# Routed attention with a SoLU layer on one core: six exponentials in w_in's place and the first part of the queues rewritten

## The chip, the cores and the metric

One core of a Trainium2 chip runs one launch. The metric is the device time in microseconds, as the median of several executions. The kernel before takes 224.04 us (three runs, 223.92 to 224.38).

## What is computed

The reference has two stages. First, attention with a mask by clusters, for 4 batches, 8 heads, 768 tokens and 64 columns per head:

```
q_assign = argmax(q_n @ c_n.T); k_assign = argmax(k_n @ c_n.T)     # 16 centroids a head
scores   = where(q_assign == k_assign, q @ k.T / 8, -1e9)
attn     = softmax(scores); x = attn @ v                            # 4 x 8 heads of 768 x 64
```

Then a feed-forward layer on x, taken as 3072 tokens of 512 columns:

```
h    = x @ w_in                                                     # 512 x 1024
solu = h * softmax(h)
out  = ((solu - mean) / sqrt(var + 1e-6) * g_ln) @ w_out            # 1024 x 512
```

## The kernel before

**How the work is tiled.** Heads are taken in 16 pairs (batch b, pair p). A pair's q and k are cast to bf16 and stored transposed, with 16 or 32 more rows under them that hold the one-hot cluster marks of each token. The product of the two then carries the score and a large constant (BIAS_C) where the clusters agree, so that one exponential gives the masked weights without a search for the maximum. Scores are made bank by bank in PSUM, 128 keys by up to 512 queries, with three banks in turn. ScalarE writes each bank's exponential as a tile e (nine buffers in turn, `ring_e` in line 1016). TensorE then multiplies e with v, which has a column of ones for the denominator, and VectorE divides. Token blocks of 128 rows, 24 in all, go through the feed-forward layer as soon as all their heads are done.

**How the order is set.** Nothing is scheduled by a program at run time. The class Weave (line 23) holds one written-out queue for each engine, `ORDER`, as a list of kinds with counts; `AWAY` names the operations that run on another engine than their usual one. Each `add` (line 98) registers an operation with its name, its engine, a cost in us, and the operations it needs. `run` (line 125) only decides in which sequence the five queues are emitted; on the chip each engine works its own queue strictly in order and waits on semaphores. So an operation that waits holds up everything behind it on its engine.

**The names**, as the steps below use them:

- `tp` (L387) TensorE transposes half of a pair's raw q (i = 0) or k (i = 1); `xa` (L394) keeps the result in SBUF (xt); `xt` (L408) is VectorE's own transpose, for batches 1 to 3.
- `ca` (L432, L434, L436) casts xt to bf16 (qk). For the first pair a cast is half a head, 64x384; for all others it is 64x768.
- `cl` (L446, L451) TensorE computes the cluster scores; `tb` (L460), `mx` (L473), `oh` (L479, L485) and `ot` (L492, L495) on VectorE make the transposed one-hot marks of them; `pl` (L507, L515) copies these marks under q and k; `bl` (L524) blanks rows.
- `S` (L602) scores, `E` (L608) exponentials, `V` (L625) the product with v, `N` (L637, L650) the division, `cv` (L533) the cast of v, `lv` (L528) its load, `ld` the loads of q and k.
- `wm` and `fl` (L820) are TensorE products of zeros that are used for nothing; `cp`, `cq` (L865) transpose the centroids.
- `li`, `wi` (L550, L553) load and cast w_in; `lo` (L566) loads w_out; `su`, `sk`, `me`, `ce` (L575, L582, L585, L588) centre w_out with g.
- for block f: `tx` (L680) transposes x, `h` (L711), `hm` (L717, row maximum), `ex` (L723), `u` (L730), `tu` (L735), `bn`, `ag` (L741, L745), `at`, `al` (L751 to L760), `y` (L775), `sc` (L790, L792), `ou` (L802).

S and E carry unit and bank: pair (0,0) is units 0 to 3, with six banks of 384 columns each (24 banks); units 4 to 21 are the other pairs of batch 0, with three banks of 512; batch 1 begins with unit 22. h3.1.0 is block 3, second half of the columns, first part. It writes over a bank that u2 reads, so it needs u2.

**The first part of the queues**, with the kinds spelled out:

```
PE   wm tp0.0.0.0 tp0.0.1.0 cp tp0.0.0.1 cl0.0.0 tp0.0.1.1 fl x5 cl0.0.1 fl x4 S0.0 S0.1 S0.2 tp0.1.0.0
     tp0.1.0.1 S1.0 S1.1 tp0.1.1.0 S1.2 cq S0.3 tp0.1.1.1 S0.4 S0.5 tp0.2.0.0 tp0.2.0.1 S1.3 S1.4
     V0.0 V0.1 V0.2 S1.5 cl0.1 S2.0 ...
ACT  wa xa0.0.0.0 xa0.0.1.0 ca0.0.0.0.0 ca0.0.0.1.1 xa0.0.1.1 ca0.0.1.0.1 ca0.0.1.1.0
     E0.0-0.2 E1.0-1.2 E0.3-0.5 E1.3-1.5 xa0.2.1.0 xa0.2.1.1 E2.0-2.5 xa0.3.0.0 E3.0 ...
DVE  cn cb xa0.0.0.1 ca0.0.1.0.0 tb0.0.0 mx0.0.0 oh0.0.0 ot0.0.0 pl0.0.0.1.1 pl0.0.0.0.0 tb0.0.1 mx oh ot
     xa0.1.0.0 xa0.1.0.1 xa0.1.1.0 bl0.0.1 cf cv0.0.0 xa0.1.1.1 zo xa0.2.0.0 xa0.2.0.1 tb0.1 ca0.1.1.0
     mx0.1 oh0.1 gk N0 ot0.1 tb0.2 ...
POOL po z1 ca0.0.0.0.1 ca0.0.0.1.0 pl0.0.0.1.0 pl0.0.0.0.1 cv0.0.1 z2 bl0.0.0 ...
SP   ld0.0 x4 lv0.0 si ld0.1.0 ld0.1.1 ld0.2.0 ld0.2.1 lv0.1 lg ld0.3.0 ld0.3.1 ld1.0 x2 lv0.2 lv0.3 ...
```

The tile w_in_sb (line 536) is filled by `wi` only after 38 us. Before that its first columns, 0 to 255 of rows 0 and 1, hold the index pattern for the identity matrix and the normed centroids (lines 812 and 841).

Of the kernel before, what the change touches and what calls it, by code (L numbers as in the profile page):

```python
# [11 lines left out]
BF16 = mybir.dt.bfloat16  # L12
# [10 lines left out]
class Weave:  # L23
# [18 lines left out]
    """
    ORDER["PE"] = """
        wm tp2 cp tp cl tp fl5 cl fl4 S3 tp2 S2 tp S cq S tp S2 tp2 S2 V3 S cl S tp2 V3 S gt S tp S
        tp S2 cl S2 V2 S V S2 tp S2 tp S2 V2 S V S2 cl S2 V2 S V2 S3 V S2 V2 S2 V S cl S3 su S2 V3 S
        V S3 V3 S2 V S su S2 V S V3 S3 me S3 V4 S3 cl S3 V4 S2 h S h S2 h S h S2 V3 S2 V h S h V S V
        S h S V S V S h S2 V3 S2 V h S2 h V2 S y3 S2 h3 S3 y V3 h V S2 V2 S cl S3 h2 S2 V3 S y2 S V
        h2 S V y2 S h S V h S2 h S y3 S2 y V3 h S3 cl V2 S V S y S2 y2 S3 V3 S y S2 V3 S2 cl S V S2
        V2 S h S2 V2 S V S h S2 V2 cl V2 S3 y2 S V S2 V y S2 y V2 S3 h2 S V h S h S2 V h S V S V y2
        S h V y2 S2 V S h3 S cl V S2 V2 S h V cl S3 h2 V y V S3 y2 V S h V3 S y S h S2 h2 S3 V2 y h  # L50
        S V S2 y V3 y S3 h3 y S3 V3 S h S V S V cl S V S h S cl V2 S3 y V2 S y S2 y V2 S3 h y V S3 V
        h V2 S3 cl S2 V2 S y3 S2 y S V3 S V S y S2 V S V3 S2 y2 S3 y V2 S2 h V2 S3 h3 S V S2 V y S V
        h2 V2 S y S2 y V y S h2 S3 cl h V S2 V3 S h V2 S3 h2 S y S2 V h S2 V y2 V4 S3 y h S2 h V h V
        S V S y2 S3 V3 h2 S2 h2 S2 y2 S V S h2 S V3 S2 h S h S2 V S y V2 S V y2 S2 h2 S2 h2 V2 S2 V2
        y S2 h V2 h V S2 h S V h S3 V2 h y S V y3 V h3 S2 y3 S2 y h2 V2 h y h y3 h V h V y4 h ptx h
        y4 h2 y3 h2 y ptu2 y6 ptu y ptu y5
    """
    ORDER["DVE"] = """
        cn cb xa ca tb mx oh ot pl2 tb mx oh ot xa3 bl cf cv xa zo xa2 tb ca mx oh gk N ot tb pl mx
        xa2 oh xa cv N ot tb pl N xt mx xt N oh ot tb pl2 ca N pl xt mx N sk oh N ot xt ce3 N tb ce5  # L60
        N hm mx N u oh ot bn N bn ag hm xt2 u N bn2 hm ag sc xt u N bn tb hm mx bn oh ag u xt bn ot
        xt N cv hm bn ag sc xt tb mx N u xt oh ot sc N bn2 xt ag xt tb N hm mx tb N oh ot u xt mx N
        bn oh bn xt hm ot ag N cv u bn2 xt hm tb mx u N tb oh mx hm ot bn2 oh ag u N sc ag hm bn ot
        u bn N xt2 ag xt2 hm tb N bl mx tb bn2 oh u N xt ag xt sc hm ot tb mx oh N bn sc N u bn N ag
        xt ot bn ca N mx sc oh hm u bn ag N xt hm bn2 bl tb u ot ag N hm mx bn2 u bn N oh ot hm bl2
        u ag N cv hm sc bn u N hm ag bn N bn u bn2 hm ag2 N bn u bn2 N ag hm bn u N ag hm bn2 u bn2
        hm sc u N ag2 bn tx hm bn sc u bn ag hm bn tu ag u2 bn2 ag sc
    """
    ORDER["ACT"] = """
        wa xa2 ca2 xa ca2 E12 xa2 E6 xa E58 ex E12 ex E8 ex E8 ex E3 sc E5 ca E2 ex E25 ex E9 sc E6  # L70
        ex E5 sc E2 ex E9 ex E8 ex E9 sc E6 ex E18 ex E21 ex E5 sc E3 ex E9 ex E7 sc E2 ex E7 ex E8
        ex E7 ex E6 sc E ex E2 sc E3 ex E2 sc ex sc ex sc ex tu sc tu2 sc2 oz
# [97 lines left out]
def kernel(  # L170
# [328 lines left out]
    def place(b, p, hf, i, part, e):  # L499
# [6 lines left out]
        if apart(b, p):  # L506
            ins = VEC[e].tensor_copy(  # L507
                side(b, p, i, part, slice(0, S))[D:D + NC_].bitcast(F32)
                .rearrange("p (t u n) -> p u t n", t=n_t // 2, u=2),
                asg[b, p, hf, "oht"][r.start:r.start + NC_].bitcast(F32)  # L510
                .rearrange("p (u t n) -> p u t n", t=n_t // 2, u=2))
        elif e == "SP":
            ins = nc.sync.dma_start(out=dst, in_=src.unsqueeze(1).to_broadcast([NB, 2, n]))
        else:
            ins = VEC[e].tensor_copy(dst.bitcast(F32), src.bitcast(F32).unsqueeze(1)  # L515
                                     .to_broadcast([NB, 2, n // 2]))
# [76 lines left out]
    es, sps_, opss, xs = {}, {}, {}, {}  # L593

# [10 lines left out]
    def expo(n, k):  # L605
        w = wide(n, k)
        es[n, k] = ep.tile([P, 512], BF16, name="e")
# [203 lines left out]
    load_v(0, 0)  # L811
# [47 lines left out]
    for j in range(sum(int(x or 1) for x in re.findall(r"\bfl(\d*)", wv.ORDER.get("PE", "")))):  # L859
# [41 lines left out]
    for idx, (b, p) in enumerate(pairs):  # L901
# [18 lines left out]
        for i in range(2):  # L920
# [340 lines left out]
```

## Time and profile before

| what | value |
|---|---|
| median of three runs | 224.04 us |
| the execution that was profiled | 223.91 us |
| its span, from first to last instruction | 221.9 us |
| granted TensorE clock | 1.00 |
| TensorE matmul busy | 213.1 us (96%) |
| VectorE busy | 197.2 us (89%) |
| ScalarE busy | 191.7 us (86%) |
| GpSimd busy | 127.1 us (57%) |

Busy shares are averages over stages with different limits. A busy TensorE is not a TensorE at its peak, since the ends of its pipelined matmuls are modelled. A row of the timeline reads: start, length, engine, line, operation, what is written and read, how many instructions were merged, and in brackets how long the engine sat idle before and what it waited for.

### The profile page before, as it was taken

The page shows a single profiled execution, that of the slowest core. Times are in us where ns is not written, and L with a number is a line of the kernel's source. Part 1 is how long each engine was busy: PE and PEld are TensorE (multiplying, and loading weights), DVE is VectorE, ACT ScalarE, POOL GpSimd, SP SyncE. Part 2 cuts the span into 40 slices and gives each one's busy share as a digit, 9 for nine tenths or more (in the row PEclk, how much of TensorE's full clock was granted, in tenths as well). Part 3 has the DMA queues.
Part 4 walks back from the last instruction along what each step waited for, and adds up shares of the span by engine and source line. Part 5 has one row for each costly group of instructions (what it writes and reads, how often), then busy time and mean ns, then how long its engine had stood idle before and what let it go on. Part 6 is the DMA issues. An engine that isn't in the chain of part 4 may idle for free.

```text
span 221.9 us, 6576 instructions
## 1 busy us (share of the span) xinstructions
PE 213.1 (96%) x2388; PEld 146.3 (66%) x2420; DVE 197.2 (89%) x359; ACT 191.7 (86%) x372; POOL 127.1 (57%) x247
## 2 busy tenths in 40 slices
PE   7899999999999999999999999999999999999994
PEld 2575656677667678776577666777677777755452
DVE  3899898899999999999998999887999889888982
ACT  3689999999899999998889899999899998983363
POOL 3499842954794999547668534953895403022331
PEclk9999999999999999999999999999999999999999
DMA  6997999999897989899999898499930524396723
GB/s 150 337 324 157 244 226 296 277 237 161 141 214 134 218 140 168 193 193 173 187 240 150 153 184 207 90 171 240 227 74 11 97 57 135 85 136 166 177 80 142
DMA packets 125679, 38.80 MB, mean 175 GB/s; under 512 B 115016, under 2 KB 121168, under 8 KB 125648
## 3 DMA queue, kind: packets, MB, share of 16 engines
q1 hardware_dynamic: 123904, 37.87, 80.4%
q10 hardware_dynamic: 1744, 0.52, 1.0%
q8 instruction: 19, 0.31, 0.6%
q14 instruction: 12, 0.10, 0.1%
HBM read 23.11 MB, written 6.29 MB: 132 GB/s over the span
## 4 chain that ended last, share of the span: by engine, by line
PE 83%; ACT 6%; issue 3%; DVE 2%; DMA 2%; POOL 1%; SPq 1%; ACTq 0%; DVEq 0%; POOLq 0%
PE sps L602 27%; PE hreg L711 17%; PE yps L775 17%; PE ops L625 13%; ACT e L608 5%; PE csc L451 4%; DMA raw<-in_q_dram 2%; PE hreg L387 1%; PE hreg L575 1%; PE hreg L775 1%; PE csc L446 1%; DVE u L730 1%; SPq L370 0%; PE utp L699 0%; ACT xt L394 0%
## 5 line engine op out<-in xcount | busy, mean ns | idle before, releaser
L608 ACT ACTIVATE e<-sps 128x512 bf16<-128x512 f32 (+1 forms) x294 | 150.7, 601 | 11.6 <-PE sps L602 9.6
L602 PE MATMUL sps<-qk 80*128 80x256 bf16 (+5 forms) x636 | 94.2, 264 | 2.0 <-POOL qk L515 0.7
L602 PEld LDWEIGHTS <-qk 80*128 80x128 bf16 (+1 forms) x636 | 60.3, 121 | 28.3 <-issue 9.2
L625 PEld LDWEIGHTS <-e 128*128 128x128 bf16 x1152 | 49.2, 97 | 12.3 <-issue 1.9
L625 PE MATMUL ops<-v,e 128*128 128x65 bf16 x1152 | 53.5, 193 | 0.1
L711 PE MATMUL hreg<-w_in_sb,xT 128*128 128x512 bf16 x173 | 49.1, 379 | 1.1
L775 PE MATMUL yps<-w_out_c,uT 128*128 128x512 bf16 x171 | 46.6, 379 | 0.6
L730 DVE TENSOR_TENSOR u<-e_sb,hreg 128x1024 bf16<-128x1024 bf16 (+1 forms) x25 | 29.1, 1168 | 4.8 <-ACT e_sb L723 4.5
L515 POOL COPY qk<-oht 32x384 f32<-32x384 f32 (+1 forms) x50 | 24.4, 488 | 15.6 <-DVE oht L495 13.4
L741 DVE BATCH_NORM_STATS2 bs<-u 128x6 f32<-128x512 bf16 x48 | 31.5, 677 | 0.1
L717 DVE TENSOR_REDUCE nmax<-hreg 128x1 f32<-128x1024 f32 x24 | 29.0, 1208 | 2.5 <-PE hreg L711 2.2
L723 ACT ACTIVATE e_sb<-hreg,nmax 128x1024 bf16<-128x1024 f32 x24 | 26.9, 1123 | 4.5 <-DVE nmax L717 4.4
L434 POOL CAST qk<-xt 64x768 bf16<-64x768 f32 (+1 forms) x31 | 25.9, 837 | 4.8 <-DVE xt L394 3.3
L775 PEld LDWEIGHTS <-uT 128*128 128x128 bf16 x200 | 18.2, 97 | 11.7 <-issue 0.3
L757 POOL TENSOR_SCALAR esq<-es,mv 128x1 f32<-128x1 f32 x24 | 8.5, 355 | 28.9 <-DVE mv L745 20.7
L436 POOL TENSOR_SCALAR qk<-xt 64x768 bf16<-64x768 f32 (+1 forms) x28 | 22.8, 815 | 1.7
L711 PEld LDWEIGHTS <-xT 128*128 128x128 bf16 x192 | 16.7, 97 | 9.5 <-DVE u L730 0.6
L408 DVE STREAM_TRANSPOSE xt<-raw 128x768 f32<-128x768 f32 x24 | 22.7, 953 | 0.2 <-DMA w_g<-in_moe_w_out_dram 0.2
L751 POOL TENSOR_SCALAR es<-esum 128x1 f32<-128x1 f32 x24 | 5.3, 222 | 27.5 <-ACT e_sb L723 27.0
L650 DVE TENSOR_TENSOR x<-ops,den 128x256 bf16<-128x256 f32 (+1 forms) x39 | 19.0, 486 | 1.3
L760 POOL TENSOR_TENSOR alpha<-esq,halves 128x1 f32<-128x1 f32 x24 | 13.5, 561 | 2.0
L533 POOL CAST v<-vf 128x384 bf16<-128x384 f32 x27 | 13.5, 516 | 0.9 <-DMA vf<-in_v_dram 0.2
(80 smaller groups left out, 165.6 us busy)
## 6 DMA issues: line engine op xcount, KB each, us to landing
vf<-in_v_dram SPq DMA_DIRECT2D x16, 384.0 KB, 4.7
out_dram<-y SPq DMA_DIRECT2D x23, 256.0 KB, 2.6
raw<-in_q_dram SPq DMA_DIRECT2D x50, 96.0 KB, 3.3
raw<-in_k_dram SPq DMA_DIRECT2D x50, 96.0 KB, 2.9
w_g<-in_moe_w_out_dram SPq DMA_DIRECT2D x4, 512.0 KB, 4.6
w_st<-in_moe_w_in_dram SPq DMA_DIRECT2D x4, 512.0 KB, 5.9
raw<-in_q_dram SPq DMA_DIRECT2D x3, 384.0 KB, 6.2
raw<-in_k_dram SPq DMA_DIRECT2D x3, 384.0 KB, 6.7
```

The lines of the kernel that those rows point to most:

```text
L434: VEC[e].tensor_copy(dst, src)
L436: VEC[e].tensor_scalar(dst, src, scalar1=inv_C, scalar2=1.0, op0=Alu.mult, op1=Alu.mult)
L515: ins = VEC[e].tensor_copy(dst.bitcast(F32), src.bitcast(F32).unsqueeze(1) .to_broadcast([NB, 2, n // 2]))
L602: nc.tensor.matmul(sps_[n, k][:, c0:c0 + w], side(b, h // 2, 1, h % 2, keys)[r], side(b, h // 2, 0, h % 2, slice(s0 * P, s0 * P + w))[r])
L608: nc.scalar.activation(es[n, k][:, :w], sps_[n, k][:, :w], Act.Exp, scale=exp_scale, bias=-exp_scale)
L625: nc.tensor.matmul(opss[g][:, s, :VW], es[n, k][:, c0:c0 + P], v1[slot(b, h // 2)][:, h % 2, kt, :VW], start=(kt == 0), stop=(kt == n_t - 1))
L711: uses(nc.tensor.matmul(hreg[:, at(f, f2)[1], :], xTs[f][:, dc, :], w_in_sb[:, dc, f2 * FF2:(f2 + 1) * FF2], start=(dc == 0), stop=(dc == ...
L717: uses(nc.vector.tensor_reduce(ff[f, "nmax"][:], pair_of(f), axis=AXY, op=Alu.max, negate=True), *both(f))
L723: uses(nc.scalar.activation(ff[f, "e"][:], pair_of(f), Act.Exp, bias=ff[f, "nmax"][:], accum_out=ff[f, "esum"][:]), *both(f))
L730: uses(nc.vector.tensor_tensor(ff[f, "u"][:, at_], ff[f, "e"][:, at_], pair_of(f)[:, at_], op=Alu.mult), *banks)
L741: nc.vector.bn_stats(ff[f, "bs"][:, f2, :], ff[f, "u"][:, f2, :])
L775: ins = nc.tensor.matmul(dst, ff[f, "uT"][:, at(f, f2)[0] * (n_fc // 2) + c, :], w_out_c[:, fc, cols], start=(fc == chunks[0]), stop=(fc = ...
```

## The change

The tiles, the shapes and the arithmetic of all operations stay as they are. Five things change.

1. **Six exponentials outside the ring.** The first six E (E0.0 to E0.2, E1.0 to E1.2) are written into free columns 256 to 1023 of rows 0 to 2 of w_in_sb. The nine buffers serve the seventh and later ones, so the sixteenth E is the first that needs an earlier V; before it was the tenth. Each `wi` now also needs `cp`, `cq` and the V of units 0 and 1.
2. **First casts and marks shared out anew.** `place` can run on ScalarE. Before the first score, ScalarE now does two of the first four marks and two casts, in place of four casts; GpSimd does the other two marks, and VectorE none. Later in the head VectorE is given casts that GpSimd did.
3. **Narrower needs.** S of the first pair with keys kt = 0 needs only the first key mark of its half, with kt = 2 only the second. S0.0 is registered after all `fl`, `gs` after all `fl`.
4. **v later or sooner on SP.** lv0.0 leaves the code ahead of the queues and comes after four ld; the others follow one at a time between ld.
5. **New order up to about 60 us** in each queue; behind it the lists are the same word for word (from S26.2 on TensorE, E26.2 on ScalarE, N11 on VectorE, at2 on GpSimd, ld2.0.0.1 on SP).

The new first part of the queues:

```
PE   fl wm fl tp0.0.0.0 fl cp tp0.0.1.0 fl x4 cl0.0.0 tp0.0.0.1 fl tp0.0.1.1 fl cl0.0.1 tp0.1.0.0 S0.0 S0.1 S0.2
     cq tp0.1.0.1 S1.0 tp0.1.1.0 S1.1 tp0.1.1.1 S1.2 S0.3 tp0.2.0.0 S0.4 tp0.2.0.1 S0.5 S1.3 tp0.2.1.0 S1.4
     cl0.1 S1.5 S2.0 V0.0 S2.1 tp0.2.1.1 S2.2 V0.1 S2.3 V0.2 S2.4 V1.0 S2.5 gt V1.1 V1.2 cl0.2 S3.0 ...
ACT  wa xa0.0.1.0 ca0.0.0.0.0 ca0.0.1.0.0 xa0.0.0.1 xa0.0.1.1 pl0.0.0.1.0 pl0.0.0.0.1
     E0.0-0.2 E1.0-1.2 E0.3-0.5 E1.3 ca0.0.0.0.1 E1.4 E1.5 E2.0-2.2 xa0.2.1.0 xa0.2.1.1 E2.3-2.5 E3.0-3.5
     E4.0-4.2 xa0.3.1.1 E5.0 ... E26.1 ca1.1.0.0 E26.2
DVE  cn xa0.0.0.0 cb ca0.0.0.1.0 tb0.0.0 mx oh ot0.0.0 ca0.0.1.0.1 tb0.0.1 mx xa0.1.0.0 oh ot xa0.1.0.1
     xa0.1.1.0 xa0.1.1.1 pl0.0.1.0.1 cf xa0.2.0.0 xa0.2.0.1 tb0.1 mx0.1 ca0.1.1.0 oh0.1 gk ca0.1.1.1 N0 ot0.1
     tb0.2 pl0.1.0.0 xa0.3.0.0 xa0.3.0.1 mx0.2 oh0.2 xa0.3.1.0 N1 ot0.2 tb0.3 cv0.1.1 ca0.2.1.0 N2 ...
POOL sg z1 zo po ca0.0.1.1.0 ca0.0.0.1.1 pl0.0.0.0.0 pl0.0.0.1.1 bl0.0.0 ca0.0.1.1.1 pl0.0.1.1.0 ...
SP   ld0.0 x4 si ld0.1.0 ld0.1.1 ld0.2.0 ld0.2.1 lv0.0 ld0.3.0 ld0.3.1 lg lv0.1 ld1.0 lv0.2 ld1.0 x2 lv0.3 ...
     ... li3 tx0 tx2 ld1.2 x2 lv1.0 ld1.2 x3 lv1.1 ...
```

Between ot0.1 and u2 the VectorE queue swaps one xa for another, gains cv0.1.1, ca0.2.1.0, cv0.3.0, ca1.0.0.0, cv0.3.1, ca1.0.1.0, ca1.0.1.1 and ca1.1.0.1, and loses cv0.2.0, pl0.2.1.1, pl0.3.0.0 and pl0.3.0.1.

The diff, with the queues and lists cut to a few lines:

```diff
     ORDER["ACT"] = """
-        wa xa2 ca2 xa ca2 E12 xa2 E6 xa E58 ex E12 ex E8 ex E8 ex E3 sc E5 ca E2 ex E25 ex E9 sc E6
...
+        wa xa ca2 xa2 pl2 E10 ca E5 xa2 E12 xa E49 ex E10 ex E6 ca E4 ex E8 ex E3 sc E5 ca
...
+        elif e == "ACT":
+            ins = nc.scalar.copy(dst, src.unsqueeze(1).to_broadcast([NB, 2, n]))
...
+    n_lent = 6
+    assert all(wide(*nk) <= HALF for nk in BANKS[:n_lent])
...
-        es[n, k] = ep.tile([P, 512], BF16, name="e")
+        i = BANKS.index((n, k))
+        es[n, k] = (w_in_sb[:, i // 2, 2 * P + i % 2 * HALF:2 * P + (i % 2 + 1) * HALF]
+                    if i < n_lent else ep.tile([P, 512], BF16, name="e"))
...
-    load_v(0, 0)
...
-            add(f"lv{t}", "SP", 0.0, -1990, lambda e: None, [], last_ld[-1:], move=1.3)
+            add(f"lv{t}", "SP", 0.5, first - 34, lambda e: load_v(0, 0), [], ["si"], move=1.3)
...
-            hots = [(i, part) for i in (1, 0) for part in range(2)]
+            hots = ([(1, 0), (0, 0), (0, 1), (1, 1)] if half and not hf else
+                    [(i, part) for i in (1, 0) for part in range(2)])
...
-                   for part in ((hh,) if apart(b, p) else range(2))}
+                   for part in ((hh,) if apart(b, p) else range(2))
+                   if not (halves_of(b, p) and x and kt % 3 == 2 * (1 - part))}
...
-            (lambda e, n=n, k=k: scores(n, k)), nd, ["S{}.{}".format(*BANKS[i - 1])] if i else [])
+            (lambda e, n=n, k=k: scores(n, k)), nd,
+            ["S{}.{}".format(*BANKS[i - 1])] if i else [f"fl{j}" for j in range(n_idle)])
...
-        if i >= ring_e:
+        if i >= ring_e + n_lent:
...
-        add(f"wi{dc}", "POOL", 1.04, 28 + dc, (lambda e, dc=dc: cast_w_in(dc, e)), [f"li{dc}"],
+        add(f"wi{dc}", "POOL", 1.04, 28 + dc, (lambda e, dc=dc: cast_w_in(dc, e)),
+            [f"li{dc}", "cp", "cq"] + [f"V{n}.{j}" for n in GROUPS[0] for j in range(3)],
             also={"DVE": 0.62})
```

More of the change, by code (lines that the diff above doesn't have):

```diff
@@ L52 @@
[L52 to L56, printed above, removed]
+        fl wm fl tp fl cp tp fl4 cl tp fl tp fl cl tp S3 cq tp S tp S tp S2 tp S tp S2 tp S
```

131 lines of the change are left out of this document (73 added, 58 removed).

## The prediction

> **What bounds the kernel now.** I read the shares of the page first, then the chain that ended last, then busy time by stretches that I cut where the limits change.
>
> ```profile
> PE 213.1 (96%) x2388; PEld 146.3 (66%) x2420; DVE 197.2 (89%) x359; ACT 191.7 (86%) x372; POOL 127.1 (57%) x247
> ...
> PE 83%; ACT 6%; issue 3%; DVE 2%; DMA 2%; POOL 1%; SPq 1%; ACTq 0%; DVEq 0%; POOLq 0%
> ```
>
> ```profile
> 0.00:9.68 9.68, 7.39 (x44) 3.59 (x45) 5.11 (x21) 4.79 (x9) 3.60 (x17) 1.00 0.83 224
> ...
> 18.30:26.50 8.20, 7.89 (x110) 5.21 (x109) 7.38 (x16) 7.92 (x19) 7.25 (x13) 1.00 0.82 190
> 26.50:44.00 17.50, 16.96 (x221) 10.42 (x220) 15.84 (x32) 16.62 (x33) 10.40 (x15) 1.00 1.03 258
> 44.00:65.20 21.20, 20.60 (x254) 15.29 (x256) 20.38 (x34) 20.22 (x41) 13.93 (x25) 1.00 1.01 190
> 65.20:120.00 54.80, 54.26 (x606) 38.60 (x615) 52.49 (x90) 51.02 (x99) 38.93 (x70) 1.00 0.99 182
> 18.30:65.20 46.90, 45.45 (x580) 30.92 (x583) 43.59 (x80) 44.75 (x91) 31.58 (x52) 1.00 0.98 215
> ```
>
> The columns are the stretch, its length, then busy PE, PEld, DVE, ACT and POOL. Up to 9.68 us nobody is full: it is one dependent chain from the load of q and k to the first score. From there ScalarE paces (7.92 of 8.20, then 16.62 of 17.50). From 44 us on PE, DVE and ACT are all full: DVE idles 0.82 us of 21.20, PE 0.60. So a lead won in the head reaches the end only if both PE and DVE carry it through 44 to 65 us, where the queues become the old ones. Behind that PE has no idle time to give back and its order is unchanged, so the lead that it has at 65 us is the gain.
>
> **Part 1, the first score (lead 0.05 to 0.3 us, taken 0.2).**
>
> ```profile
> 6.26 0.53 PE L451 MATMUL csc<-xt,c_bd 128*32 128x192 f32 x8
> ...
> 6.37 0.56 DVE L394 COPY xt<-hreg 128x384 f32<-128x384 f32 x1 [0.37 <-PE hreg L387]
> ...
> 6.84 0.34 DVE L436 TENSOR_SCALAR qk<-xt 64x384 bf16<-64x384 f32 x1
> ...
> 7.11 0.37 DVE L460 STREAM_TRANSPOSE cst<-csc 128x192 f32<-128x192 f32 x1
> ...
> 7.88 1.06 ACT L432 ACTIVATE qk<-xt 64x384 bf16<-64x384 f32 x2
> ...
> 8.77 0.58 DVE L515 COPY qk<-oht 32x192 f32<-32x192 f32 x2
> 8.88 0.75 POOL L515 COPY qk<-oht 32x192 f32<-32x192 f32 x2 [0.77 <-DVE oht L495]
> ...
> 9.68 0.65 PE L602 MATMUL sps<-qk 80*128 80x384 bf16 x3 [0.72 <-POOL qk L515]
> ```
>
> tb0.0.0 starts at 7.11, 0.32 after its matmul's end at 6.79, because an xt copy and a cast stand ahead of it on DVE. Both are done earlier or elsewhere in the new queue, so tb starts near 6.82: 0.29 won. The marks then cost more: today two on DVE and two on POOL end at 9.63, 0.89 after ot. Now S0.0 needs two marks on ScalarE, and two ScalarE copies of that length took 1.06 (7.88), so 1.06 + 0.07 for the semaphore after ot: 0.24 lost. If they pipeline as the exponentials do (0.38 apart) the loss is gone. Bounds 0.05 and 0.3; I take 0.2. The extra `fl` ahead of the first transposes cost nothing, since cl0.0.0 waits for the k half that lands near 5.0.
>
> **Part 2, the exponentials of the first pair (lead 0.7 to 1.5 us at E5.0, taken 1.3).**
>
> ```profile
> 10.04 3.56 ACT L608 ACTIVATE e<-sps 128x384 bf16<-128x384 f32 x9 [1.11 <-PE sps L602]
> 14.30 1.26 ACT L608 ACTIVATE e<-sps 128x384 bf16<-128x384 f32 x3 [0.71 <-PE ops L625]
> 15.94 0.86 ACT L394 COPY xt<-hreg 128x384 f32<-128x384 f32 x2 [0.38 <-PE hreg L387]
> ...
> 22.12 2.12 ACT L608 ACTIVATE e<-sps 128x512 bf16<-128x512 f32 x4
> ```
>
> Nine exponentials run, then the tenth waits 0.71 for the V that frees the ring. With six more places that wait goes. E4.0 starts at 22.12. In the new queue: E0.0 at 9.84, 24 exponentials at 0.38 (nine took 3.56) are 9.12, the cast in between 0.53 (half of 1.06), the two xt copies 0.8: E4.0 at 20.3. One xt copy (0.45) has moved behind it, so the lead is 1.8 - 0.45 = 1.35, about 1.3 at E5.0. S4.0 must then be ready by 20.1; it needs ot0.1, which part 3 puts at 18.05 to 19.0, and a mark after it. That is just reached, so any slip there shortens the lead; 0.7 is what the ring's wait alone gives.
>
> **Part 3, VectorE's longer queue (costs 0 to 4 us, taken 2.3).** Between ot0.1 and u2 it gains five casts and three v casts, and loses one v cast and three marks.
>
> ```profile
> L436 DVE TENSOR_SCALAR qk<-xt x3: 344/530/610, 6.8 to 147.5; 64x768 bf16<-64x768 f32 x2, 64x384 bf16<-64x384 f32 x1
> L434 DVE CAST qk<-xt x1: 742/742/742, 33.5 to 33.5; 64x768 bf16<-64x768 f32 x1
> L533 DVE CAST v<-vf x5: 359/451/568, 13.0 to 174.6; 128x384 bf16<-128x384 f32 x5
> L507 DVE COPY qk<-w_out_c x5: 351/354/878, 20.0 to 34.8; 16x384 f32<-16x384 f32 x5
> ```
>
> Added: 5 x 0.60 (between 0.53 and 0.74) and 3 x 0.45, 4.35 us. Removed: 0.45 + 0.35 + 0.88 + 0.35, 2.03. Net 2.3. Against it stands DVE's idle time, 46.90 - 43.59 = 3.31 us, of which these waits could go:
>
> ```profile
> DVE den L637 <- PE ops L625: 0.9, 3, 0.4
> DVE cst L460 <- PE csc L451: 0.4, 1, 0.4
> DVE u L730 <- ACT e_sb L723: 0.4, 1, 0.4
> DVE w_sum L582 <- PE hreg L575: 0.3, 1, 0.3
> DVE xt L408 <- DMA w_g<-in_moe_w_out_dram: 0.2, 1, 0.2
> ```
>
> That is 2.2 us, all waits for engines that would now be earlier. So the added work about fills the holes. ot0.1 starts at 18.29 today. In the new queue N0, two instructions before it, waits for V1.2, and that for E1.5 and S2.5; by part 2 S2.5 is done near 16.4, and gt, gk, one cast and N0 (0.25 + 0.15 + 0.60 + 0.75) put ot0.1 at about 18.05: lead 0.25. At u2 DVE's lead is 0.25 + 2.2 - 2.3 = 0.15.
>
> ```profile
> 63.96 1.22 DVE L730 TENSOR_TENSOR u<-e_sb,hreg 128x1024 bf16<-128x1024 bf16 x1
> ...
> 65.66 1.03 PE L711 MATMUL hreg<-w_in_sb,xT 128*128 128x512 bf16 x4
> ```
>
> u2 ends at 65.18, and h3.1.0, which needs it, starts at 65.66 because PE is not sooner there. With 0.07 for the semaphore PE could come 0.41 earlier today. So PE's lead at h3.1.0 can be 0.15 + 0.41 = 0.56 and no more, although the ScalarE side would give 1.3.
>
> The casts were on POOL before; there they were hidden (31.58 busy of 46.90). At one place the trace shows how the two engines meet:
>
> ```profile
> 32.42 0.83 POOL L436 TENSOR_SCALAR qk<-xt 64x768 bf16<-64x768 f32 x1
> ...
> 33.32 0.51 POOL L533 CAST v<-vf 128x384 bf16<-128x384 f32 x1
> ...
> 33.49 0.74 DVE L434 CAST qk<-xt 64x768 bf16<-64x768 f32 x1
> ```
>
> The mark of 0.88 ended at 33.46, 0.21 after the POOL cast's end at 33.25, and the DVE cast of 0.74 ended 0.41 after POOL's v cast: each looks as if it had waited for POOL's instruction to end. Alone they would be 0.35 and 0.41. If each of the eight new copies lost 0.41 (half of a POOL cast's 0.83) to that, added work would be 5 x 0.41 + 3 x 0.36 + 8 x 0.41 = 6.4 and not 4.35. The Trainium skill, page "SBUF — State Buffer", section "Who interferes with whom", says that a vector copy or cast in a two-port mode and a GpSimd instruction exclude each other for the whole instruction, whichever came first; these rows agree with it.
>
> **Part 4, the rest.** ca1.1.0.0 (64x768) on ScalarE before E26.2 costs 0.84, by the one such cast there:
>
> ```profile
> 61.26 1.58 ACT L608 ACTIVATE e<-sps 128x512 bf16<-128x512 f32 x3 [0.65 <-PE sps L602]
> ...
> 74.72 0.84 ACT L432 ACTIVATE qk<-xt 64x768 bf16<-64x768 f32 x1
> ```
>
> ScalarE waits 0.65 for PE just behind it, and three h of 1.3 us together stand between S26.2 and S27.0, so I cost it at nothing; without that cover it is 0.2. On SP tx2, which waits for N7, now stands ahead of three loads of q and three of v:
>
> ```profile
> 41.05 1.90 SPq L400 DMA_DIRECT2D raw<-in_q_dram  x3
> 43.05 1.50 SPq L528 DMA_DIRECT2D vf<-in_v_dram  x3
> 44.63 1.68 SPq L680 DMA_TRANSPOSE xT<-x  x1
> ```
>
> The loads of batch 1's third pair start some 4.5 us later, at about 45.5. Eight issues of 0.5 then end near 50 and the last two wait for u0, to about 54; its transposes on DVE stand at 56.3 and 57.2 in the old order, later in the new one. Nothing, with 1 us as the price if the second is missed. Free columns of w_in_sb are read and written in other places at the same time (centroids up to cq); different columns, so nothing; if the E had to wait for cq, which now stands right behind S0.2, 0.3 us.
>
> **The sum.** 223.91 us, the profiled execution, - 0.56 = 223.35. The median of the three runs stands 0.13 above that execution: **223.5**. The span goes from 221.9 to 221.3.
>
> **Rivals.**
> - *The whole lead arrives.* If the moved copies cost their undisturbed 0.41 and 0.36, 3.1 us are added, 1.1 net; DVE's lead at u2 is 0.25 + 2.2 - 1.1 = 1.35 and ScalarE's 1.3 decides: 222.7. For it: POOL is less busy where the casts left. Against: DVE and POOL overlap in most of this stretch.
> - *Nothing arrives.* DVE's lead is about -0.4 and PE's spare 0.41 just covers it: 224.0. That is also what the port's exclusion gives at POOL's present share: 8 x 0.67 x 0.41 = 2.2 on top of 1.1 net, lead 0.25 + 2.2 - 3.3 = -0.85, or -0.1 where POOL's lighter queue avoids a third of it. It is the same outcome if the E in w_in_sb are tied to other users of that tile and the ring's wait comes back in another form.
> - *Slower: DVE becomes the bound at u2.* If the casts cost 0.74 each and the v casts 0.57 (5.4 added, 3.4 net) and half of the waits stay, the lead is 0.25 + 1.1 - 3.4 = -2.05; beyond PE's spare 0.41 that is 1.6 lost: 225.6 at worst, and 224.7 halfway. It decides once DVE is over 0.41 late at u2. For it: in 44 to 65 us DVE has only 0.82 to give.
>
> **Chances.** Forecast 0.42, whole lead 0.17, nothing 0.16, slower 0.25. The forecast runs from 223.1 to 223.8. A difference of 0.2% (0.45 us) is about what a measurement of this kernel can tell from none: 0.30 of the forecast and all of the whole lead are faster than that, 0.12 and the 0.16 are the same. Faster 0.47, same 0.28, slower 0.25. The range reaches from the whole lead, with a little more from part 1, to just beyond the halfway point of the slower case: 222.5 to 224.8.
>
> **What would show it.** Right: S0.0 near 9.5; no wait at the tenth exponential; E4.0 near 20.5; DVE idle in 18 to 65 us down from 3.3 to about 1; u2 and h3.1.0 both near 65.0 with hardly a gap between them. Wrong: E4.0 later than 21.4 (part 2); moved copies over 0.65 on the mean (part 3); h3.1.0 before 64.6, which would mean that DVE did not hold PE; or a wait on a transpose's load near 58 us (part 4).

## The result and the profile after

The changed kernel takes **226.25 us** (median of 22 executions, 224.43 to 228.56), the kernel before in the same comparison 224.37 (22 executions, 223.86 to 226.5). The ratio is **1.0057, 95% interval 1.0037 to 1.0077**: slower by 0.6%, where 223.5 was forecast with a range up to 224.8. Executions over 1.5% above the fastest of their kernel are left out of all ratios, here three above 228 us, though a profile of one of 229.22 us, below, shows the same kind of wait that makes the loss.

The profiled execution is one of the fastest: 224.72 us, span 222.6, clock 0.996. So there are two things to explain: 0.8 us that this profile shows against the one before (223.91), and some 1.5 us more in the typical execution (0.5 in the kernel before), which it does not show. First the shares of the chain that ended last, then the stretches:

```profile
PE 75%; POOL 8%; DVE 7%; ACT 4%; issue 3%; DMA 1%; DVEq 0%; POOLq 0%; ACTq 0%
```

```profile
44.00:65.20 21.20, 21.05 (x257) 15.15 (x255) 20.83 (x35) 20.98 (x42) 9.04 (x18) 1.00 0.95 175
...
18.30:65.20 46.90, 46.14 (x587) 32.02 (x584) 45.89 (x84) 45.14 (x91) 29.30 (x50) 1.00 0.95 207
```

VectorE's idle time from 18.30 to 65.20 us fell from 3.31 to 1.01 us, as forecast. GpSimd has 8% of the chain (1% before). Now the head, then ScalarE alone, then the hand-over at 65 us (timeline rows):

```profile
5.27 0.85 PE L394 MATMUL hreg<-ident_f,raw 128*128 128x128 f32 x3
...
6.16 0.48 ACT L401 COPY xt<-hreg 128x384 f32<-128x384 f32 x1 [1.82 <-PE hreg L394]
...
8.87 1.04 ACT L522 COPY qk<-oht 32x384 bf16<-32x384 bf16 x2 [0.22 <-DVE oht L502]
...
9.96 0.66 PE L613 MATMUL sps<-qk 80*128 80x384 bf16 x3 [0.27 <-ACT qk L522]
```

```profile
10.34 2.41 ACT L621 ACTIVATE w_in_sb<-sps 128x384 bf16<-128x384 f32 x6 [0.43 <-PE sps L613]
12.64 1.64 ACT L621 ACTIVATE e<-sps 128x384 bf16<-128x384 f32 x4
14.31 0.52 ACT L439 ACTIVATE qk<-xt 64x384 bf16<-64x384 f32 x1
14.74 2.02 ACT L621 ACTIVATE e<-sps 128x384 bf16<-128x384 f32 x5
...
18.85 3.98 ACT L621 ACTIVATE e<-sps 128x384 bf16<-128x384 f32 x9 [0.17 <-PE sps L613]
...
23.08 7.19 ACT L621 ACTIVATE e<-sps 128x512 bf16<-128x512 f32 x14
```

```profile
63.88 1.18 DVE L743 TENSOR_TENSOR u<-e_sb,hreg 128x1024 bf16<-128x1024 bf16 x1
...
65.32 1.03 PE L724 MATMUL hreg<-w_in_sb,xT 128*128 128x512 bf16 x4
...
66.70 0.18 POOL L1246 MEMSET v<- 128x96 bf16 x1
...
66.94 0.71 PE L638 MATMUL ops<-v,e 128*128 128x65 bf16 x18 [0.15 <-POOL v L1246]
```

The first score starts at 9.96 (9.68 before). The wait of 0.71 at the tenth exponential is gone, and E5.0 starts at 23.08 (23.64). u2 is 0.08 earlier and h3.1.0 0.34 earlier (65.66). Then the lead ends in one step: V28.0 starts at 66.94, where it started at 66.97 before, because it waits for a memset on GpSimd. That is z5, the column of ones of the sixth v buffer; before it ran at 15.12, and in the new GpSimd queue it stands behind al1. From there PE is level with the kernel before up to 142 us, then falls 0.2 behind (part 3 below has the row), and its last products start at 216.84 (216.68). Behind them the chain of after has a piece that no engine explains (0.05 us in the same place before):

```profile
218.82 0.42 issue
219.24 0.48 DVE e_sb L805
```

These two, 0.16 and 0.37, are most of the 0.7 by which the span is longer. The lists are the same there. In other profiles this piece is 0.40 (the repeat) or 0.05 again (SP's old order); what decides it is open.

So the profile shows a change that wins nothing. A cause for what the typical execution loses is first visible in SP's queue. These are SP's rows of after, in two windows, where the old queue issued six loads from 41.05 to 44.54:

```profile
39.96 1.33 SPq L693 DMA_TRANSPOSE xT<-x  x1
```

```profile
44.01 1.67 SPq L693 DMA_TRANSPOSE xT<-x  x1
45.76 1.10 SPq L407 DMA_DIRECT2D raw<-in_q_dram  x2
...
51.84 1.25 SPq L748 DMA_TRANSPOSE uT<-u  x1
```

From 41.29 to 44.01 SP issues nothing: tx2 waits for the division N7, and six loads stand behind it. Nine issues lie between tx0 and tu0 (51.84), eleven did before. From there the queue is hardly ever idle up to tx6 near 92 us, so what was not issued comes late all the way. tu3, the transposing DMA for y3, shows it. First its row on SP before, and from the view of uT on SP before the time from issue to landing (least, median and most of 22); then both for after:

```profile
73.90 1.50 SPq L735 DMA_TRANSPOSE uT<-u  x1
```

```profile
DMA to landing us min/median/max: 3.0/3.6/5.7
```

```profile
74.91 1.45 SPq L748 DMA_TRANSPOSE uT<-u  x1
```

```profile
DMA to landing us min/median/max: 3.0/3.4/5.0
```

y3.0 wants it at 79.4 in both kernels. Before, 73.90 + 3.6 leaves 1.9 us, and even the slowest flight of 5.7 is only 0.2 late. After, a flight of 5.0 from 74.91 is 0.5 late.

### The profile page after: what moved, and what is told of

It reads as the page before. It is cut to its first block, busy times and chain, and to the rows that moved or that the text cites. A ratio compares the mean times of both kernels' runs of the same rounds, so it can differ in the third digit from the quotient of the medians.

```text
span 222.6 us, 6604 instructions
## 1 busy us (share of the span) xinstructions
PE 216.3 (97%) x2420; PEld 147.5 (66%) x2420; DVE 198.4 (89%) x361; ACT 192.6 (87%) x374; POOL 123.7 (56%) x243
## 4 chain that ended last, share of the span: by engine, by line
PE 75%; POOL 8%; DVE 7%; ACT 4%; issue 3%; DMA 1%; DVEq 0%; POOLq 0%; ACTq 0%
PE sps L613 22%; PE yps L788 16%; PE hreg L724 15%; PE ops L638 12%; PE csc L458 4%; ACT e L621 3%; POOL qk L441 2%; POOL qk L514 2%; PE idle_p L832 2%; PE hreg L394 2%; DVE u L743 2%; DMA uT<-u 1%; POOL qk L443 1%; DVE xt L415 1%; DVE bs L754 1%
## 5 line engine op out<-in xcount | busy, mean ns | idle before, releaser
L621 ACT ACTIVATE e<-sps 128x512 bf16<-128x512 f32 (+1 forms) x288 | 148.6, 603 | 9.6 <-PE sps L613 8.5
L638 PE MATMUL ops<-v,e 128*128 128x65 bf16 x1134 | 54.5, 193 | 0.2 <-POOL v L1246 0.2
L724 PE MATMUL hreg<-w_in_sb,xT 128*128 128x512 bf16 x192 | 53.0, 379 | 0.0
L788 PE MATMUL yps<-w_out_c,uT 128*128 128x512 bf16 x184 | 48.9, 379 | 0.0
L524 POOL COPY qk<-oht 32x384 f32<-32x384 f32 (+1 forms) x49 | 24.9, 507 | 20.3 <-DVE oht L502 15.6
L441 POOL CAST qk<-xt 64x768 bf16<-64x768 f32 (+1 forms) x27 | 22.1, 819 | 2.3 <-ACT xt L401 0.9
L443 POOL TENSOR_SCALAR qk<-xt 64x768 bf16<-64x768 f32 (+1 forms) x25 | 20.2, 808 | 4.1 <-ACT xt L401 2.6
```

Source lines behind the costliest of these rows:

```text
L441: VEC[e].tensor_copy(dst, src)
L621: nc.scalar.activation(es[n, k][:, :w], sps_[n, k][:, :w], Act.Exp, scale=exp_scale, bias=-exp_scale)
L638: nc.tensor.matmul(opss[g][:, s, :VW], es[n, k][:, c0:c0 + P], v1[slot(b, h // 2)][:, h % 2, kt, :VW], start=(kt == 0), stop=(kt == n_t - 1))
L724: uses(nc.tensor.matmul(hreg[:, at(f, f2)[1], :], xTs[f][:, dc, :], w_in_sb[:, dc, f2 * FF2:(f2 + 1) * FF2], start=(dc == 0), stop=(dc == ...
L788: ins = nc.tensor.matmul(dst, ff[f, "uT"][:, at(f, f2)[0] * (n_fc // 2) + c, :], w_out_c[:, fc, cols], start=(fc == chunks[0]), stop=(fc = ...
```

## Experiments

In the diffs of SP's queue, cut to the part from tx0 on, `tx2` is tx0 and tx2 one behind the other, and the `tu` are tu0, tu1 and tu2 in this order. **Theory A**: late transposing DMAs make the loss, by SP's order. **Theory B**: the engines' order makes it.

**The changed kernel again, the old SP order, and early memsets.** The second and fourth have this edit (the fourth with the third's as well):

```diff
     ORDER["SP"] = """
...
-        tx2 ld2 lv ld3 lv ld tu ld9 lv tu tx ld lv ld4 tu
+        tx ld3 lv3 tx ld4 tu ld9 lv ld tu tx ld3 tu
...
```

and the third this one, z4 and z5 beside z2 and z3:

```diff
     ORDER["POOL"] = """
...
-        z2 ca cv ca pl3 cv pl ca cv ca gs ca2 pl6 bl z wi pl wi3 cv pl at pl al cv pl at ca bl cv pl cv ca3 al z at
+        z4 ca cv ca pl3 cv pl ca cv ca gs ca2 pl6 bl wi pl wi3 cv pl at pl al cv pl at ca bl cv pl cv ca3 al at
...
```

> The changed kernel as it is, on another chip, to see where a typical execution of it loses time. Theory A (late loads): SP's queue from 62 us on runs about 1 us behind the old one, because ld1.3.1, lv1.3 and ld2.0.0.0 now stand behind tu1 and tx4; the transposes of batch 2 had 2.6 to 2.8 us between landing and use before and have 0.9 to 2.0 in the profile of the changed kernel; in the typical execution (median 226.25 against the profiled 224.72) some DMA is later than that and PE or VectorE waits for it. Then a new profile that is 1 us or more over 222.6 in span shows waits on loads between 62 and 100 us. Theory B (compute): the loss is fixed in the engines' order (z5 behind al1, first score 0.3 later), and the scatter belongs to the machine: then the ratio stays at 1.004 to 1.008 and no load is late.

> The changed kernel with SP's queue from tx0 on in its old order (tx2 behind the first three v loads of batch 1, ld1.3.1, lv1.3 and ld2.0.0.0 ahead of tu1 and tx4); everything else as changed. Theory A (late loads): the scatter goes and the median falls by about 1.3 us, to 0.999 to 1.002 of the kernel before. Theory B: within 0.2 us of the changed kernel.

> The changed kernel with the two memsets z4 and z5 (the ones columns of the fifth and sixth v buffer) back beside z2 and z3 at about 15 us on GpSimd, instead of z5 behind al1 at 66.7 us. Theory B: V28.0 starts with h3.1.0's lead of 0.36 kept, so the time falls by 0.3 us. Theory A alone: the 0.3 is won in fast executions, but the scatter stays, so the median falls by 0.3 at most.

> Both edits, SP's old order from tx0 on and z4, z5 early. Theory A and z5 together: 1.6 us under the changed kernel, 0.2 to 0.5 us under the kernel before. Theory B without A: 0.3 us under the changed kernel, still 0.2% to 0.4% over the kernel before.

| kernel | median us | ratio to before |
|---|---|---|
| changed, again | 226.42 | 1.0103 (1.0067 to 1.0138) |
| SP's old order | 224.66 | 0.9986 (0.9959 to 1.0013) |
| z early | 228.59 | 1.0142 (1.0091 to 1.0194) |
| both | 224.74 | 0.9994 (0.9969 to 1.0019) |

Theory A holds, B falls: SP's old order takes the loss away, early memsets do not. The 0.2 to 0.5 us under the kernel before, which A expected of both edits together, did not show. The repeat was profiled in an execution of 229.22 us. PE's waits from 40 us on, SP's row for tu3, PE's row for y3.0, and the stretches behind it (the granted clock stands third from the end):

```profile
PE yps L788 <- DMA uT<-u: 1.7, 1, 1.7
PE hreg L724 <- DMA xT<-x: 1.5, 1, 1.5
```

```profile
77.16 1.50 SPq L748 DMA_TRANSPOSE uT<-u  x1
```

```profile
82.29 0.39 PE L788 MATMUL yps<-w_out_c,uT 128*128 128x512 bf16 x1 [1.68 <-DMA uT<-u]
```

```profile
82.00:84.00 2.00, 1.66 (x7) 0.94 (x9) 1.69 (x3) 0.78 (x2) 1.44 (x4) 0.80 0.76 124
84.00:86.00 2.00, 2.00 (x9) 1.14 (x8) 0.86 (x2) 0.72 (x2) 1.90 (x3) 0.50 0.95 152
86.00:88.00 2.00, 2.00 (x28) 1.71 (x27) 0.18 (x1) 1.80 (x4) 1.77 (x5) 0.85 1.06 169
```

tu3 is issued at 77.16, PE waits 1.7 us for it, and then works at a clock of 0.80, 0.50 and 0.85: (0.20 + 0.50 + 0.15) x 2 = 1.7 us more. Another 1.5 went at h0.0.0, which waited for tx0; that this one comes from the order is not shown (Left open, below). That is 4.9 us against the 4.5 by which this execution was slower than the first profile. The profile with early memsets shows the same place (2.0 us for tu3, clock down to 0.50). What z5 is worth by itself stayed hidden under that; with both edits PE keeps its lead past V28.0 (below).

**Which move in SP's queue, taken back one by one, and what a late transpose costs.** From tx0 on, in this order: tx2 back; tu1 and tx4 back; and, in the kernel before, tu3 put five loads later. The fourth is the kernel before with the six exponentials of point 1 alone (the lines of `n_lent` in its diff, without the new needs of `wi`), all queues as before.

```diff
-        tx2 ld2 lv ld3 lv ld tu ld9 lv tu tx ld lv ld4 tu
+        tx ld2 lv ld3 tx lv ld tu ld9 lv tu tx ld lv ld4 tu
```

```diff
-        tx2 ld2 lv ld3 lv ld tu ld9 lv tu tx ld lv ld4 tu
+        tx2 ld2 lv ld3 lv ld tu ld9 lv ld lv ld tu tx ld3 tu
```

```diff
-        tx ld3 tu ld3 ou ld2 ou ld tu ld12 tu
+        tx ld3 tu ld3 ou ld2 ou ld6 tu ld7 tu
```

> The changed kernel with tx2 alone put back behind the first six loads of batch 1's third pair. Theory A1 (tx2 stalls SP's queue): in the changed kernel SP issues nothing from 41.30 to 44.01 us, while tx2 waits for N7, with six loads behind it that the old queue issued from 41.05 to 44.54; the whole queue runs late from there, tu3 is issued at 74.9 to 77.2 us instead of 73.9, and y3.0 waits for it. Then the median falls to 224.5 to 225.0 (0.997 to 1.002 of the kernel before). Theory A2 (tu1 and tx4 ahead of ld1.3.1, lv1.3 and ld2.0.0.0): stays at 226 or above.

> The changed kernel with tu1 and tx4 alone put back behind ld1.3.1, lv1.3 and ld2.0.0.0; tx2 stays ahead of the loads. Theory A1: stays at 226 or above, y3.0 still late. Theory A2: falls to 224.5 to 225.0.

> The kernel before with one edit: tu3, the transposing DMA for y3, five loads later in SP's queue, about 2.8 us. It landed at 77.54 for a use at 79.4, so PE should wait about 1 us for it near 80 us. Theory C (the price of a late transpose is more than its wait): two slow executions of the changed kernel and of the one with early memsets waited 1.7 and 2.0 us for tu3, PE's granted clock then fell to 0.67 to 0.90 for some 8 us, and PE was 3.3 and 3.9 us late in all from y3.0 on; so here the clock falls too and the loss is 1.5 to 4 us. Rival: the clock fell by chance or for the other engines' reasons; then the loss is the wait alone, 0.5 to 1.2 us.

> The kernel before with the six exponentials in w_in's place and nothing else of the change: all queues in their old order. It tests the prediction's second part. Theory of the prediction: the wait of 0.71 at the tenth exponential goes, E4.0 comes 0.3 to 0.7 earlier and PE reaches h3.1.0 up to 0.4 earlier: 223.6 to 224.1 where the kernel before has 224.1. Rival: in the old order PE's own sequence (the v products stand ahead of the scores) holds the next scores, so ScalarE waits for PE instead and nothing is won: within 0.1 us.

Measured: tx2 back 1.008 (1.0048 to 1.0113); tu1 and tx4 back 1.011 (1.0068 to 1.0153); tu3 late 1.013 (1.009 to 1.017); exponentials alone 1.0008 (0.9978 to 1.0038). Neither theory of a single move came out: both kernels stay slow, and PE now waits at other places, 1.2 us for an xT near 97 us in the first and 1.1 us for tu1 in the second.

With tu3 late, it was issued at 78.37, PE waited 2.2 us for it (1 was expected), and the clock stayed at 1.00. The loss lies in the range of theory C, but not for its reason: most of it is the wait, which was longer, and the clock falls only sometimes (the last section shows when). The exponentials alone give nothing that can be told, as the rival said. ScalarE in that kernel, whose first exponential came at 10.73 (10.04 before):

```profile
13.00 2.73 ACT L612 ACTIVATE e<-sps 128x384 bf16<-128x384 f32 x6
16.62 0.86 ACT L394 COPY xt<-hreg 128x384 f32<-128x384 f32 x2 [0.89 <-PE hreg L387]
17.37 2.58 ACT L612 ACTIVATE e<-sps 128x384 bf16<-128x384 f32 x6
```

The ring's wait is gone and 0.89 us of waiting for PE's transposes stands in its place; E2.0 starts at 17.37, which is 16.68 of the kernel before and the 0.69 by which this execution began later.

**Two loads at tu0, and the casts.** The new queue has ld1.2.1.2 and lv1.2 behind tu0, which waits for u0. They go ahead of it, alone and together with tx2's old place:

```diff
-        tx2 ld2 lv ld3 lv ld tu ld9 lv tu tx ld lv ld4 tu
+        tx2 ld2 lv ld3 lv ld2 lv tu ld8 tu tx ld lv ld4 tu
```

```diff
-        tx2 ld2 lv ld3 lv ld tu ld9 lv tu tx ld lv ld4 tu
+        tx ld2 lv ld3 tx lv ld2 lv tu ld8 tu tx ld lv ld4 tu
```

The other two take SP's old order and the early memsets, and give two of VectorE's casts back to GpSimd, ahead of cv1.0.0; the last one also has the old head of PE's queue (`wm tp2 cp tp cl tp fl5 cl tp fl4 S3`):

```diff
     ORDER["POOL"] = """
...
-        wi3 cv pl at
+        wi3 ca2 cv pl at
...
     ORDER["DVE"] = """
...
-        N2 ce2 mx ce hm ca N u oh bn2 N hm ot ca ag
+        N2 ce2 mx ce hm N u oh bn2 N hm ot ag
...
+    AWAY.update({'ca1.0.1.1': 'POOL', 'ca1.1.0.1': 'POOL'})
```

> The changed kernel with two loads of batch 1, ld1.2.1.2 and lv1.2, put ahead of tu0 in SP's queue; tx2, tu1 and tx4 stay as changed. Theory A3: what costs is that SP reaches tu0, which waits for u0 until about 51.8, with two issues fewer done than in the old order (9 against 11 since tx0); from there to tx6 near 92 us the queue has no idle time, so those two issues of 0.5 to 0.6 us are 1.1 us of lateness for every transposing DMA in between. Then the median falls to 224.5 to 225.0. Rival, that one of the other moves is enough by itself to make a transposing DMA late: it stays above 225.8.

> The changed kernel with the two loads ahead of tu0 and tx2 behind the first six loads; only tu1 and tx4 (ahead of ld1.3.1, lv1.3 and ld2.0.0.0) and the order of loads among themselves stay as changed. Theory A3: as the one with the two loads alone, 224.5 to 225.0; tu3 is issued before 74.6. If tu1's and tx4's place were a cause of its own, it stays above 225.8.

> SP's old order from tx0 on, z4 and z5 early, and two of the five moved casts (ca1.0.1.1, ca1.1.0.1) back on GpSimd, where it idles from 44 to 51 us. Theory D (VectorE is the bound behind 44 us): with SP and z repaired, N12 on VectorE was 0.16 earlier than before and PE's 0.39 at h3.1.0 fell to 0.24 at h4.0.0; two casts of 0.6 off VectorE lift its lead at u2 to 0.8 to 1.3, PE keeps 0.3 to 0.4 (ScalarE's lead) to the end: 0.996 to 0.999 of the kernel before. Rival: the lead goes at another place behind 65 us all the same, and the ratio is that of SP and z alone, 0.999 to 1.001.

> As the one with the two casts back on GpSimd, and the head of PE's queue in its old order: no idle matmul ahead of the first transposes, cp behind the second. Theory: the changed head put S0.0 at 9.96 instead of 9.68, since the extra idle matmuls and cp held tp0.0.1.0 until 5.27 (5.04 before) and ScalarE's copy of it until 6.16 (5.60 before); with the old head S0.0 comes 0.3 earlier, and E4.0 and ScalarE with it: 0.2 to 0.4 us below the one without it, 0.995 to 0.998 of the kernel before. Rival: 0.3 in the head is taken up before 65 us by VectorE's queue, no difference.

Two loads alone: 1.0064 (1.0018 to 1.0111), with a median of 228.30 us, a miss for the theory of the two loads; here PE waits 3.2 us for tu0. Both moves taken back: 1.0023 (0.9987 to 1.0059) and 225.55 us, between the two expectations; its interval holds no loss as well as most of it. Casts: **0.9956 (0.9932 to 0.9981)**. With the old head on top 0.9989 (0.9961 to 1.0018): no gain from it; in its profile k's half came at 5.32 us (5.04 before), so the head hangs on the landing of a load, and this run cannot tell the two orders apart.

**One part alone, added.** The kernel before with the new SP order from tx0 on (the first diff of all, the other way round); SP's old order (second kernel above) with tx2 alone moved, and with tu1 and tx4 alone moved; and the kernel with the casts again.

```diff
-        tx ld3 lv3 tx ld4 tu ld9 lv ld tu tx ld3 tu
+        tx2 ld3 lv3 ld4 tu ld9 lv ld tu tx ld3 tu
```

```diff
-        tx ld3 lv3 tx ld4 tu ld9 lv ld tu tx ld3 tu
+        tx ld3 lv3 tx ld4 tu ld8 tu tx ld lv ld4 tu
```

> The same kernel as the one with SP's old order, early memsets and two casts back on GpSimd, run again for the interval and for an undisturbed profile (its first one waited 2.3 us for tu0 near 56 us). Theory D: 0.994 to 0.999 of the kernel before again, and in the profile VectorE's lead at N12 is 0.8 or more and PE's lead of 0.3 to 0.4 lasts to the end. Rival: 0.999 to 1.002, the first ratio was the luck of the executions.

> The kernel before with SP's queue from tx0 on in the changed order, and nothing else of the change: the other side of the run with SP's old order. Theory A (the SP order alone makes the loss): 225.5 to 227, 1.006 to 1.012 of the kernel before, with waits of PE for an uT or xT load in the profile. Rival (the order costs only together with the engines' new order): within 0.2% of the kernel before.

> The kernel with SP's old order from tx0 on, with tx2 alone ahead of the six loads of batch 1's third pair. Theory A1 (one stall of SP is enough): SP idles from about 41.3 to 44.0, stays 1 us or more late to 92 us, 225.5 or more. Theory A4 (margins add up: no single move is the cause, each takes 0.5 to 1 us of a margin of about 2 us): between 224.6 and 225.6, some executions at 226 and over.

> The kernel with SP's old order from tx0 on, with tu1 and tx4 alone ahead of ld1.3.1, lv1.3 and ld2.0.0.0. Theory A4: as the old order within 0.2%, since the three loads are only exchanged with two transposing DMAs and tx4's wait for x4 is 0.4 us: 224.3 to 225. Theory A2 (their place is a cause): 225.5 or more.

| kernel | median us | ratio to before |
|---|---|---|
| casts, again | 223.90 | 0.9977 (0.9962 to 0.9993) |
| before, with the new SP order | 226.12 | 1.0065 (1.0032 to 1.0098) |
| old SP order, tx2 alone moved | 227.08 | 1.0121 (1.0094 to 1.0148) |
| old SP order, tu1 and tx4 alone moved | 224.65 | 1.0012 (0.9998 to 1.0026) |

The new SP order alone makes a loss of the same size in the old kernel. Within it tx2's place is enough, and tu1's and tx4's place costs nothing that can be told. But in the profile of the old kernel with the new SP order the loss lies at other places. PE's longest waits there, and VectorE's that stands behind the first of them:

```profile
PE hreg L711 <- DVE u L730: 1.3, 1, 1.3
PE hreg L711 <- DMA xT<-x: 1.0, 1, 1.0
```

```profile
DVE xt L408 <- POOL v L533: 1.5, 1, 1.5
```

The 1.0 is tx0 again. The 1.5 is a transpose of batch 1's third pair, which starts at 60.10. The view names a cast on GpSimd, which ended last in this profile, but VectorE's queue waited until 60.02, when the last load of k of this pair landed. That load stands behind tu0 and was issued at 55.50 (53.54 before), with a flight of 4.5 us (2.4). VectorE's u1 and PE's h2.1.0 came late by it. So the stall can be paid at the load's own user as well; this is the wait near 58 us that the prediction named as a sign.

SP's rows with tx2 alone moved, and then PE's wait and clock:

```profile
43.60 1.78 SPq L692 DMA_TRANSPOSE xT<-x  x1
45.47 1.67 SPq L406 DMA_DIRECT2D raw<-in_q_dram  x3
47.24 1.50 SPq L536 DMA_DIRECT2D vf<-in_v_dram  x3
48.79 0.46 SPq L406 DMA_DIRECT2D raw<-in_q_dram  x1
49.35 4.22 SPq L406 DMA_DIRECT2D raw<-in_k_dram  x3
53.67 1.24 SPq L747 DMA_TRANSPOSE uT<-u  x1
```

```profile
57.88 1.04 PE L787 MATMUL yps<-w_out_c,uT 128*128 128x512 bf16 x4 [1.95 <-DMA uT<-u]
```

```profile
58.00:60.00 2.00, 2.00 (x19) 1.37 (x18) 1.07 (x2) 0.00 (x0) 1.84 (x5) 0.69 1.03 165
60.00:62.00 2.00, 2.00 (x16) 1.26 (x14) 0.00 (x0) 1.08 (x2) 1.81 (x4) 0.50 1.10 175
```

All ten loads behind tx2's wait are squeezed in ahead of tu0, which goes out at 53.67 (52.25 before) and makes PE wait 1.95 us. So the stall at tx2 makes tu0 late here, and where two loads are left behind tu0, as in the changed kernel, the later transposes. With tx2 back and the two loads still behind tu0, tu3 was still issued at 76.09 (73.90 before), without the stall. This fits that neither move brought the time back by itself.

The kernel with the casts is the best of all, and its gain reaches the end. Its stretch, u2, h3.1.0 and the last products:

```profile
44.00:65.20 21.20, 21.06 (x258) 15.16 (x256) 20.03 (x34) 20.98 (x42) 10.49 (x19) 1.00 0.99 191
```

```profile
63.61 1.19 DVE L742 TENSOR_TENSOR u<-e_sb,hreg 128x1024 bf16<-128x1024 bf16 x1
```

```profile
65.17 1.03 PE L723 MATMUL hreg<-w_in_sb,xT 128*128 128x512 bf16 x4
```

```profile
216.33 1.91 PE L787 MATMUL hreg<-w_out_c,uT 128*128 128x256 bf16 x16
```

VectorE has 1.17 us to spare from 44 to 65 us, u2 is 0.35 earlier than before, h3.1.0 0.49, and the last products 0.35 (216.68 before); the median is 0.49 lower. For VectorE 0.8 or more was expected. (The two intervals overlap with that of SP and z alone, 0.9969 to 1.0019; it is the profile that shows where the difference comes from.) Its first profiled execution still lost 2.3 us to a late tu0, which also happens in the old SP order now and then.

## Why the prediction was wrong

**The step that failed is part 4**, "Nothing, with 1 us as the price if the second is missed". It followed the three loads of q and three of v to their own users, the transposes of batch 1's third pair, and in the profiles of the changed kernel VectorE does not wait for them. (In the kernel before with the new SP order it does, for 1.5 us: there the price that part 4 named came due.) It did not follow the stall to what is queued behind on SP: tu0, tu1, tu3, tx6. In the repeat tu3 was issued 3.3 us later than before and cost 3.4 us with the fall of the clock. tu3's margin of 1.9 us and the flights of 3.0 to 5.7 were to be read in the trace of before. SP's order alone is worth 1.0065, as much as was lost. It also took the 0.13 us between execution and median as fixed; the order made the median 1.5 us worse than the profiled execution.

**Part 1** (0.2 won): S0.0 came 0.28 later, not 9.5. ScalarE's two marks took 1.04 as forecast. "The extra fl ahead of the first transposes cost nothing" did not fit: PE came to the second transpose only at 5.27, and ScalarE's copy followed at 6.16 (5.60). But over the profiles the first exponential starts at 9.71 to 10.60 with the new head (thirteen) and at 10.04 to 11.11 with the old one (four), so the head's loss is no more than the spread.

**Part 2** (1.3 at E5.0): the wait of the ring went, as said; E4.0, the seventh of the nine from 18.85, came near 21.2, inside the 21.4 named as the limit, and the lead at E5.0 was 0.56, under the bound of 0.7. The late head took 0.3 of it: counted from the first exponential, E5.0 comes after 12.74 us instead of 13.60, a lead of 0.86. The run with the exponentials alone shows that the ring's wait by itself was worth nothing, since PE's order took its place.

**Part 3** was right in mechanism and nearly in size. These are the groups of the moved copies in 18.3 to 65.2 us (mean ns of one behind the busy time), against 600 and 450 forecast:

```profile
L441 DVE CAST qk<-xt 64x768 bf16<-64x768 f32 x3 | 2.0, 650 | 0.0
L443 DVE TENSOR_SCALAR qk<-xt 64x768 bf16<-64x768 f32 x3 | 1.9, 649 | 0.0
L542 DVE CAST v<-vf 128x384 bf16<-128x384 f32 x3 | 1.5, 500 | 0.0
```

5 x 0.65 + 3 x 0.50 - 2.03 = 2.7 for 2.3, and u2 is 0.08 earlier for 0.15. Two of the six took 0.84 and 0.86 us and the others 0.53 to 0.56, so 0.3 was added to two copies and not 0.41 to each. These two end 0.42 and 0.41 after a GpSimd copy's end (26.18 and 34.51), as the rows of the prediction have it: the exclusion came, but for two of six. What failed is the next line, "the lead that it has at 65 us is the gain", said of PE. Its lead of 0.34 was mostly its spare, and it did not last. With z5 early and SP's old order, these are u2, h3.1.0 and the last products:

```profile
63.84 1.18 DVE L742 TENSOR_TENSOR u<-e_sb,hreg 128x1024 bf16<-128x1024 bf16 x1
```

```profile
65.27 1.03 PE L723 MATMUL hreg<-w_in_sb,xT 128*128 128x512 bf16 x4
```

```profile
216.59 1.91 PE L787 MATMUL hreg<-w_out_c,uT 128*128 128x256 bf16 x16
```

0.39 at h3.1.0 has become 0.09 at the end, in two steps. ScalarE's ex3 waits for VectorE's hm3, which is 0.16 earlier and no more, and PE has 0.24 left from h4.0.0 on. From 139 us on another 0.15 goes. This second step stands in all fourteen profiles with the new first part and in none of the four with the old one, though the lists are the same there. In the changed kernel it is this wait of ScalarE, which the kernel before does not have:

```profile
138.82 1.57 ACT L621 ACTIVATE e<-sps 128x512 bf16<-128x512 f32 x3 [0.28 <-PE sps L613]
```

This exponential starts 0.14 after the second score ahead of it ends (138.68); before, it starts at 138.56, 0.08 after the first one (138.48). Why it waits for one score more is open. So that VectorE's 0.12 at u2 comes near the 0.09 of the end is chance in part. z5 behind al1, which cost the rest at 67 us in the changed kernel, was not in the prediction at all; it listed GpSimd's casts, not the memsets that the new order moved.

**The rivals.** Of the three, "nothing arrives" describes what the profiled execution won, but not why: VectorE was 0.08 early at u2, not 0.4 late. The slower rival had the right sign and the wrong place: VectorE was not late at u2. What was found, a stall in SP's queue that the loads behind pass on, was no rival; part 4's "1 us" and its sign near 58 us come nearest.

**Left open:** why one DMA flies 3 us and the next 5; why tx0 landed 5.7 to 7.1 us after its issue in five profiles and 3.1 to 4.4 in the other thirteen (three of the five have tx0 and tx2 in their old places, so the order is not shown to be the cause); why ScalarE waits for one score more near 139 us; and how the loss divides between tx2 and the two loads in the executions of the changed kernel that have no profile.

## What to carry to other kernels

When a waiting DMA moves ahead of others in one queue, follow everything behind it up to the queue's next idle time, and set each item's margin against the longest flight that the profile shows, not the median. A lead is worth no more than what every engine in the chain behind it carries; the slack of one of them is spent once. And word-for-word equal lists behind a change can still run with other waits. One profiled execution can be among the best of a kernel: where margins are about the spread of a DMA's flight, the median of many is another number.

## What the runs showed of the hardware

- The granted clock fell to 0.50 after PE gaps of 1.68, 1.95 and 2.05 us, for 3.4 us each time (the lost 1.7 us at half speed), and stayed at 1.00 after gaps of 2.16, 2.34 and 3.20 us in other runs. So a wait of under 2 us can cost as much again, and the length of the gap alone did not decide. In these traces the clock changes in whole steps of 3.413 us: with tx2 alone moved it rose at 4.17, fell at 58.78, rose at 62.19 and fell at 226.03, which is 16, 1 and 48 steps. Laid on this grid, the three gaps that cost the clock lie whole within one step (55.93 to 57.88 in the step that ends at 58.78, and likewise for the repeat at 83.19 and early memsets at 81.77). The three others lie across a boundary: 56.55 to 59.75 across 58.21 (two loads), 80.68 to 82.84 across 82.05 (tu3 late), 56.96 to 59.30 across 58.49 (casts), so no step had more than 1.66 us of them. That the idle time within one step decides fits all six, but no run moved a gap along the grid on purpose, and at the end of the last kernel (casts, again) 1.9 us of a step behind PE's last product did not lower the clock. The Trainium skill, page "TensorE: Matmul & The Clock Gate", section "Part 1: The HAM clock gate", has the clock halve after an idle window of some 3.4 us that runs free of the program. The 3.4 us at half speed agree with its window; that a whole window must be idle does not, since 1.68 us were enough.
- SP mostly needs 0.5 us to issue a load, yet in the kernel before 12 of the 122 loads of q, k and v took over 1.1 us or up to 2.9 each, and in the run above three loads of k took 4.22 us together (at 49.35). A queue that looks as if it had room has less than its count of issues says.
